# Attention with landmarks and a SiLU layer on one core: first loads reordered, two turns moved, a cast split, a new plan

## The chip, the core and the metric

The kernel runs on one core of a Trainium2 chip. Time is device time in microseconds (us) of one launch on that core, input and output in the chip's memory. The core has five engines that work in parallel, each strictly through its own list of instructions: TensorE (PE, matrix products, with a separate track PEld for weight loads), VectorE (DVE), ScalarE (ACT), GpSimd (POOL) and SyncE (SP, here only transfers). Where an engine's next instruction waits on a semaphore, everything behind it on that engine waits too.

## The reference

```python
batch, n_heads, seq, head_dim = (8, 8, 576, 64)      # q, k, v
n_tokens, d_model, d_ff = (4608, 512, 2048)          # w_in, w_out
q_lm = q.reshape(B, H, m, S // m, D).mean(axis=3)    # m = 32 landmarks, S // m = 18
k_lm = k.reshape(B, H, m, S // m, D).mean(axis=3)
A  = sm(q, k_lm)          # softmax over scale * a @ b^T
Bm = sm(q_lm, k_lm)
C  = sm(q_lm, k)
Z  = Bm^T / (norm1(Bm) * norminf(Bm) + 1e-06)
for _ in range(6):
    Z = 2 * Z - Z @ Bm @ Z
x = A @ Z @ C @ v         # per head; heads side by side: 512 columns
h = x @ w_in
out = (h * sigmoid(h)) @ w_out
```

All of it in float32; the kernel works in bfloat16 with float32 sums.

## The kernel before, in words

The eight batches run one after the other, overlapped. For each batch the kernel loads q, k and v (casting to bf16 on the way), sums 18 rows into each landmark (`landmarks`), turns q and k so that the head dimension lies on partitions (`turn`), and makes the three score matrices (`scores_b`, `scores_c`, `scores_a`). exp(C) (`pc`) is transposed to `pt` and multiplied by v (`values`); six Newton steps (`steps`, `steps_x`) with that product give z (`z_of`, tile `zt`). `mix` multiplies z by w_in into M (tile `m`), which is cast from PSUM; so the wide product x @ w_in is A^T times M (`layer1`, PSUM tiles h0 and h1, SiLU by ACT). `layer2` multiplies by w_out in tiles of 128 rows, 16 products each, into o0 and o1; ACT copies each to `ost` and SP stores it.

No list of instructions is written by hand. Every step is a node of a plan (class `_Plan`, L37) with an engine, a cost, a priority and the nodes it depends on; the planner goes through time and gives each engine, of the nodes it holds to be ready, the one with the lowest priority number. `SHIFT` (L21) adds to priorities by name and batch. `FLAGS` (L26) says which engine takes a step: letters D, A, P stand for DVE, ACT, POOL, E for TensorE, S for ACT in two halves. The lists so made are fixed in the program; on the chip the real times count, not the planner's.

What the change touches:

- Loads. All go through POOL (`load_w_in` L359, `load_w_out` L370, `load` L378). The first ones follow the list `FIRST` (L30, walked at L1124): k, q, v of batch 0, quarter 0 of w_in (w01), k and q of batch 1, the rest of w_in (w12, w24), the four slabs of w_out (o0 to o3), v of batch 1. An issue waits until the load eight places earlier has landed, and POOL waits with it. In the program that was built, batch 1's q stands before its k, and the slabs of w_out come right after w24.
- A's softmax in `top_a` (L652), `exps_a` (L695) and `weights_a` (L987): each of two halves (512 and 640 columns) gets a maximum on DVE, a subtraction on DVE or POOL (L663), exp on ACT (L706), a sum and reciprocal on DVE, a product on POOL or DVE (L1004, the norm) and a transpose on DVE into `at` (L1008). For batch 0 the 640 subtraction and both norms are POOL's.
- `turn` (L477): for batches 0 to 3 four DVE transposes (L488, L495); for batches 4 to 7 two transfers on SP's queue (L481), first q then k. From batch 4 on exp(C) is also turned by SP (L792).
- `mix` (L942): for batch 0 chunk 0 goes through h0, chunks 1 to 3 through o0 and o1, and each chunk is cast by two DVE instructions (L975).
- `landmarks` (L404): 'E' sums by 18 products with the identity on PE and one cast; else POOL adds a tree of five (L442). From batch `ts` = 4 on the tree waits for the subtractions of the batch before.
- PE's lists are filled with `layer2` products wherever the planner sees room.

Of the kernel before, what the change touches and what calls it, by code (L numbers as in the profile page):

```python
# [19 lines left out]

SHIFT = {'DVE gx t 3': 2.5, 'DVE qT qn 3': -0.5, 'DVE lmT lm 3': 3.5, 'PE t gx 3': 3, 'DVE crec csum 3': -0.25, 'DVE asum ea 0': -0.5, 'POOL kn 1': -0.5, 'DVE at ea 3': 2, 'DVE asum ea 2': 2.5, 'ACT ea s 3': 1.0, 'PE t qn 0': -1, 'DVE bs t 3': -2.5, 'POOL qn 3': -1, 'DVE m h 0': -1.75, 'POOL kn 3': -1.0, 'POOL bmd bm 0': -0.25, 'POOL kn 2': -3.0, 'DVE pt h 1': 2, 'PE t gx 2': -1, 'PE t xp 0': -0.25, 'PE t lmT 1': 0, 'ACT ea s 1': 1, 'ACT xp h 0': -2, 'PE t bt 1': 2, 'ACT lm h 2': 0.5, 'DVE bm t 3': 0.25, 'DVE m h 1': 1, 'PE t gc1g 0': 0.5, 'DVE cmax h 2': 0.25, 'PE h m 0': -2, 'DVE bsum t 1': -0.25, 'PE o g 0': 0.5, 'DVE at ea 2': 0.5, 'PE o g 2': 2, 'DVE kT kn 0': -1, 'POOL bmd bm 2': 1, 'PE t lmT 2': 0.5, 'DVE n t 1': -2, 'PE t kn 0': 1, 'DVE at ea 0': 3, 'POOL vn 1': 2, 'PE h m 2': -0.25, 'PE o lmT 0': 1, 'PE h pt 1': -0.5, 'DVE rn n 2': 2, 'PE o g 1': 2, 'DVE gc0t t 1': 0.5, 'PE t lmT 3': -0.5, 'PE t bt 0': 0.25, 'ACT ost3b o 3': 0.25, 'PE h zt 0': 1, 'DVE lmT lm 2': -2, 'DVE n t 2': 1, 'POOL qn 1': -0.5, 'DVE bt gc0t 1': 2, 'DVE brec bsum 1': -0.25, 'DVE cneg cmax 3': -1, 'ACT t bs 2': -1, 'DVE bmax t 2': -1.25, 'POOL bmd bm 3': -0.25, 'DVE gc0g t 1': 0.25, 'POOL ea arec 2': 2, 'POOL tree kn 3': 2, 'DVE lmT lm 1': -2.5, 'POOL qn 0': -0.25, 'DVE gc1g t 1': 0.25, 'DVE bs t 2': 1.0, 'DVE bsum t 3': 0.5, 'DVE n t 5': -0.25, 'PE t qn 1': 0.5, 'DVE bm t 7': -1, 'PE h pc 0': -0.25, 'PE t kn 1': -0.5, 'DVE s h 6': -2, 'DVE bmax t 7': -0.5, 'ACT pc h 6': 0.5, 'PE h lmT 3': -1, 'PE t bm 3': 0.75, 'DVE rn n 1': 0.0, 'DVE bt bm 2': 0.25, 'DVE amax s 7': -0.5, 'ACT pc h 1': -0.5, 'POOL qn 4': -0.5, 'DVE pt h 2': -1.75, 'DVE kT kn 2': -0.5, 'DVE pt h 4': 0.25, 'DVE n t 3': 1, 'DVE bmd t 0': -2, 'DVE bs t 1': 1, 'ACT m h 5': 1, 'DVE bmax t 1': -2, 'ACT ost o 7': 1, 'DVE crn crec 0': -0.5, 'PE t gc0t 1': 1.0, 'PE t xp 2': -1.5, 'PE t gx 5': 2, 'DVE gx t 2': 1, 'PE o g 3': 2, 'DVE pt h 7': -1, 'DVE crec csum 7': -1, 'PE h zt 3': -1, 'DVE rn n 3': 1, 'PE t gx 6': 1, 'ACT t bs 5': -1, 'POOL kn 4': 0.25, 'DVE at ea 1': 1, 'DVE bt bm 3': 2, 'ACT g h 1': 0.5, 'ACT ost o 0': 0.5, 'ACT ost3b 7': -2, 'DVE qT qn 2': -2, 'ACT m h 4': -0.5, 'DVE at ea 4': -2, 'PE h m 3': -1, 'DVE arec asum 2': -1, 'DVE ident s 0': 1, 'DVE xp gx 2': 1, 'PE t gc1g 1': -2, 'POOL tree qn 6': 1, 'DVE asum ea 6': 0.5, 'DVE gd gx 5': 2, 'DVE kT kn 3': 0.25, 'DVE crn crec 1': 0.25, 'PE h zt 2': 0.5, 'PE t gx 7': -2, 'PE t gc0t 0': 2, 'ACT t bs 3': -0.25, 'ACT g h 2': 2, 'DVE btd bt 4': 2, 'POOL lm tree 3': 0.5, 'DVE gc0g t 0': 1, 'POOL tree 3': -2, 'PE o g 5': 1, 'ACT t bs 1': 0.25, 'ACT ost o 2': 0.5, 'DVE qT qn 0': 1, 'DVE s o 1': -2, 'POOL tree qn 5': 2, 'DVE arec asum 3': 2, 'DVE cneg cmax 6': 2, 'DVE brec bsum 0': -0.25, 'ACT lm t 0': -2, 'ACT ea s 2': 2, 'ACT ea s 5': -2, 'DVE gd gx 2': -0.5, 'DVE asum ea 5': 2, 'POOL ea arec 1': 2}  # L21

FLAGS = {'st0': 'DDDAAA', 'st1': 'DAAADD', 'pt0': 'SS', 'pt1': 'AA', 'sub0': 'DP', 'sub1': 'DP', 'mul0': 'PP', 'mul1': 'PD', 'lm1': 'EE', 'lm2': 'EE', 'lz': 1, 'tb': 4, 'ts': 4, 'gb': 2, 'pb': 4}  # L26
TB, PB, GB = FLAGS['tb'], FLAGS['pb'], FLAGS['gb']


FIRST = ['k0', 'q0', 'v0', 'w01', 'k1', 'q1', 'w12', 'w24', 'o0', 'o1', 'o3', 'o2', 'v1']  # L30

XM = 0.21

# [180 lines left out]
def kernel(  # L214
# [143 lines left out]

    def load_w_in(lo, hi):  # L359
        def f():  # L360
            for qd in range(2):
                G.dma_start(
                    out=w_in_sb[64 * qd:64 * qd + 64, :, 512 * lo:512 * hi],
                    in_=moe_w_in[256 * qd:256 * qd + 256,
                                 512 * lo:512 * hi].rearrange(
                        "(h d) f -> d h f", d=D))
        return P.add("POOL", 1.4, f, w=[f"w_in{c}" for c in range(lo, hi)],
                     dma=[1.3 * (hi - lo)] * 2, prio=-5)

    def load_w_out(ci):  # L370
        def f():
            G.dma_start(
                out=w_out_sb[:, 4 * ci:4 * ci + 4, :],
                in_=moe_w_out[512 * ci:512 * ci + 512, :].rearrange(
                    "(c p) f -> p c f", p=128))
        P.add("POOL", 0.7, f, w=[f"w_out{ci}"], dma=[2.6], prio=-0.5)

    def load(t, src, b):  # L378
        if t == "v":
            def f():  # L380
                for t3 in range(3):
                    G.dma_start(  # L382
                        out=nat[t][b % 2][32 * t3:32 * t3 + 32].rearrange(
                            "p h j d -> p h (j d)"),
                        in_=src[b].rearrange("h (l t j) d -> t l h (j d)",
                                             t=3, j=6)[t3])
            P.add("POOL", 2.0, f, w=[f"{t}n{b % 2}"], dma=[0.95] * 3,
                  prio=-5 if b == 0 else -0.5)
            return
# [4 lines left out]
        def f():  # L394
            G.dma_start(out=dst, in_=rows.rearrange("(c p) n -> p c n", p=128))  # L395
        P.add("POOL", 0.75, f, w=[f"{t}n{b % 2}"],
              dma=[2.8], after=gate, prio=-5 if b == 0 else -0.5)


    HALF = ((0, 8), (8, SEG))  # L400
    TS = FLAGS["ts"]
    subs = {}

# [73 lines left out]
    def turn(b):  # L477
        p2 = b % 2
        if b >= TB:
            for t, dst in (("k", kTd), ("q", qTd)):  # L480
                P.add("SP", 2.3, lambda t=t, dst=dst: nc.sync.dma_start_transpose(  # L481
                    out=dst.rearrange("p a i n -> p (a i) n"),
                    in_=nat[t][p2].rearrange("p a i d -> p (a i d)")),
                    r=[f"{t}n{p2}"], w=[f"{t}T.0", f"{t}T.1"], prio=-1, lat=4.7)
            return
        for qd in range(2):
            def f(qd=qd):
# [3 lines left out]
                        "p (t c) w -> p t c w", c=6))  # L491
            dve(576, f, r=[f"kn{p2}"], w=[f"kT.{qd}"], prio=3 if b else 0.2)
        for qd in range(2):
            def f(qd=qd):
# [3 lines left out]
                        "p i w -> p (i w)"))  # L498
            dve(576, f, r=[f"qn{p2}"], w=[f"qT.{qd}"], prio=3 if b else 0.9)

# [431 lines left out]

    def copy_m(b, ci):
        dst = m_sb[b % 2][:, :, 512 * ci:512 * ci + 512]
        if ci % 2:
            dve(1024, lambda: V.tensor_copy(out=dst, in_=h_ps[1]), r=["h1"],  # L936
                w=[f"m{b % 2}.{ci}"], prio=0.1)
        else:
            act(1024, lambda: A.copy(out=dst, in_=h_ps[0]), r=["h0"],  # L939
                w=[f"m{b % 2}.{ci}"], prio=-1)  # L940

    def mix(b):  # L942

        p2 = b % 2
        for ci in range(4):
# [27 lines left out]
            if b == 0 and ci:  # L973
                for qd in range(2):
                    dve(512, lambda qd=qd, dst=dst, tgt=tgt: V.tensor_copy(  # L975
                        out=dst[:, qd], in_=tgt[qd]), r=[ks[qd]],
                        w=[f"m{p2}.{ci}"], prio=1)
            else:
# [8 lines left out]
    def weights_a(b):  # L987

        a3 = b % 3
        for hf, (i0, i1) in enumerate(HALF):  # L990
# [15 lines left out]
                    2).to_broadcast((128, 2 * (p1 - p0), LM, 2)), op=OP.mult),  # L1006
                r=[f"arec{hf}"], w=[f"ea{hf}"], prio=0.92 if on_dve else -1)
            dve(n // 2, lambda ev=ev, p0=p0, p1=p1: V.transpose(  # L1008
                out=at_sb[a3][:, :, p0:p1].bitcast(FP).rearrange(
# [5 lines left out]
    def layer1(b, part=range(NDC)):  # L1015
# [5 lines left out]
        if b == 0:  # L1021
            for hf, (i0, i1) in enumerate(HALF):
                t0, t1 = 32 * i0, 32 * i1
                n = t1 - t0
                for d2 in range(NDC // 2):
                    hp = h_ps[d2 % 2]

                    def f(d2=d2, hp=hp, t0=t0, t1=t1, n=n):
                        for j in range(2):
                            dc = 2 * d2 + j  # L1030
                            for qd in range(2):
# [3 lines left out]
                    pe(4 * _mm_cost(n), f, r=([f"m0.0{d2}d", f"m0.0{d2}a"] if d2 < 2 else  # L1035
                                               [f"m0.{d2 // 2}"]) + [f"at{a3}.{hf}"],
                       w=[f"h{d2 % 2}"], mode="full", prio=1, ni=8, hold=1)
# [84 lines left out]
    for b in range(B):  # L1122
        loads += [("k", k, b), ("q", q, b), ("v", v, b)]
    for n, x in enumerate(FIRST):  # L1124
        if n == 2:
            constants()
        if x[0] == "w":
            load_w_in(int(x[1]), int(x[2]))
        elif x[0] == "o":
            load_w_out(int(x[1]))  # L1130
        else:
            load(*loads[3 * int(x[1]) + "kqv".index(x[0])])
    for step in SEQ:
# [5 lines left out]
        if step[0] in "ES":  # L1139
# [6 lines left out]
            else:  # L1146
# [12 lines left out]
                weights_a(b)  # L1159
                z_of(b)  # L1160
        if step[0] in "EX":
            if b:
# [56 lines left out]
```

## Time and profile before

| | |
|---|---|
| three runs | 264.89, 265.57, 266.40 us, median 265.57 |
| profiled execution | 266.55 us |
| its span, first to last instruction | 264.8 us |
| mean granted TensorE clock | 0.971 |
| PE busy | 243.5 us (92%) |
| ACT, DVE, POOL busy | 161.6, 149.9, 124.1 us |
| written by DMA | 35.03 MB, mean 132 GB/s |
| `layer2` products, 555 recorded | 133.7 us |
| `layer1` products of 288, 512 recorded (with two other shapes) | 76.5 us |

The three runs lie within 0.6% of each other. The profiled execution is 0.98 us above the median. PE is the engine that is nearly always busy; from 235.5 us to the end it does nothing but `layer2`. In the lines below, a row of the timeline has the start in us, the duration, engine, line, operation, tiles, shape and count, and in brackets how long the engine stood idle before and what ended that.

### The profile page before, as it was taken

How to read it: one execution, taken by the hardware profiler on the slowest of the kernel's cores; microseconds unless marked ns; L12 is line 12 of the kernel's file. 1: busy time of each engine (PE TensorE's matmuls, PEld its weight loads, DVE VectorE, ACT ScalarE, POOL GpSimd, SP SyncE). 2: the span in 40 equal slices, each digit the busy share in tenths (PEclk: the TensorE clock that was granted, in tenths of full speed). 3: DMA queues.
4: the chain of work that ended last, by engine and by line, in shares of the span. 5: the costliest groups of instructions: out<-in, count | busy, mean ns of one | idle time of the engine just before them, and what ended most of it. 6: DMA issues, size and time to landing. Idle time of an engine off the chain costs nothing.

```text
span 264.8 us, 6634 instructions
## 1 busy us (share of the span) xinstructions
PE 243.5 (92%) x2702; PEld 138.4 (52%) x2739; DVE 149.9 (57%) x394; ACT 161.6 (61%) x275; POOL 124.1 (47%) x141
## 2 busy tenths in 40 slices
PE   5868799999799999999999989998999999999993
PEld 3733455644564466445744556435743664654452
DVE  4696853888994995486548644596369723000000
ACT  2173379843986588658865966386769786861111
POOL 8525617949431599259943995189422300000000
PEclk9985799999999999999999999999999999999998
DMA  6999999999596867188995999894215111013334
GB/s 95 198 202 211 206 209 207 207 223 222 97 174 120 136 126 129 40 167 181 165 198 108 179 169 214 144 180 98 59 40 102 42 41 42 0 40 78 72 69 102
DMA packets 47838, 35.03 MB, mean 132 GB/s; under 512 B 29248, under 2 KB 38720, under 8 KB 47808
## 3 DMA queue, kind: packets, MB, share of 16 engines
q0 software_dynamic: 14624, 18.35, 41.4%
q1 hardware_dynamic: 33104, 16.19, 30.8%
q8 instruction: 21, 0.34, 0.5%
q10 hardware_dynamic: 80, 0.07, 0.1%
q14 instruction: 9, 0.07, 0.1%
HBM read 36.70 MB, written 9.44 MB: 174 GB/s over the span
## 4 chain that ended last, share of the span: by engine, by line
PE 68%; DMA 12%; POOL 6%; DVE 5%; issue 4%; ACT 3%; ACTq 0%; POOLq 0%; DVEq 0%
PE o L244 39%; PE h L244 27%; DMA w_in_sb<-in_moe_w_in_dram 7%; DMA vn<-in_v_dram 3%; PE t L244 3%; POOL tree L442 3%; DMA lmdT<-lmd 2%; DMA pt<-pc 1%; POOL vn L382 1%; DVE cmax L587 1%; DVE pt L809 1%; ACT ost L1086 1%; ACT g L1055 1%; DVE s_sb L640 1%; POOL qn L395 1%
## 5 line engine op out<-in xcount | busy, mean ns | idle before, releaser
L244 PE MATMUL o<-w_out_sb,g 128*128 128x512 bf16 (+1 forms) x555 | 133.7, 373 | 3.3 <-issue 2.1
L244 PEld LDWEIGHTS <-g 128*128 128x128 bf16 x592 | 52.7, 98 | 52.5 <-issue 7.9
L1055 ACT ACTIVATE g<-h 128x576 bf16<-128x576 f32 x112 | 67.6, 651 | 17.4 <-PE h L244 17.2
L244 PE MATMUL h<-at,m 128*128 128x288 bf16 (+2 forms) x512 | 76.5, 290 | 1.5 <-DVE pt L809 0.8
L244 PEld LDWEIGHTS <-m 128*128 128x128 bf16 x512 | 49.4, 99 | 26.4 <-issue 2.9
L1086 ACT COPY ost<-o 128x512 f32<-128x512 f32 (+1 forms) x37 | 21.2, 573 | 45.1 <-PE o L244 44.6
L663 POOL TENSOR_TENSOR s_sb<-s_sb,amax 128x640 f32<-128x640 f32 (+1 forms) x14 | 16.2, 1170 | 47.7 <-DVE amax L657 46.7
L442 POOL TENSOR_TENSOR tree<-tree 128x512 f32<-128x512 f32 (+2 forms) x30 | 24.5, 816 | 2.0
L936 DVE CAST m<-h 128x1024 bf16<-128x1024 f32 x14 | 17.1, 1218 | 13.5 <-PE h L244 8.9
L1004 POOL TENSOR_TENSOR ea<-ea,arec 128x512 bf16<-128x512 bf16 (+1 forms) x15 | 17.0, 1147 | 9.3 <-DVE arec L999 9.3
L939 ACT CAST m<-h 128x1024 bf16<-128x1024 f32 x14 | 14.2, 1012 | 7.5 <-PE h L244 7.3
L906 DVE SCALAR_TENSOR_TENSOR gx<-gx,t 128x192 bf16<-128x192 bf16 x30 | 10.5, 352 | 13.2 <-PE t L244 13.0
L706 ACT ACTIVATE ea<-s_sb 128x512 bf16<-128x512 f32 (+1 forms) x16 | 13.0, 845 | 4.7 <-POOL s_sb L663 4.1
L712 DVE TENSOR_TENSOR gd<-gx,t 128x256 bf16<-128x256 bf16 x36 | 15.1, 419 | 1.2
L382 POOL DMA_DIRECT2D vn<-in_v_dram x24 | 14.1, 593 | 1.3 <-PE t L244 1.0
L587 DVE TENSOR_REDUCE cmax<-h 128x1 f32<-128x576 f32 x16 | 11.8, 749 | 4.1 <-PE h L244 4.0
L1038 ACT ACTIVATE g<-h 128x512 bf16<-128x512 f32 (+1 forms) x16 | 9.8, 648 | 6.9 <-PE h L244 6.9
L688 ACT ACTIVATE pc<-h,cneg 128x576 bf16<-128x576 f32 x16 | 11.7, 733 | 3.6 <-DVE cneg L590 3.5
L995 DVE TENSOR_REDUCE asum<-ea 128x16 f32<-128x512 bf16 (+1 forms) x16 | 11.8, 742 | 1.5 <-ACT ea L706 1.4
L442 POOL TENSOR_TENSOR tree<-qn 128x1152 f32<-128x1152 bf16 x5 | 11.9, 2375 | 0.9 <-DMA qn<-in_q_dram 0.7
L442 POOL TENSOR_TENSOR tree<-kn 128x1152 f32<-128x1152 bf16 x5 | 11.9, 2372 | 0.0
L657 DVE TENSOR_REDUCE amax<-s_sb 128x16 f32<-128x512 f32 (+1 forms) x16 | 11.3, 733 | 0.0
(124 smaller groups left out, 258.1 us busy)
## 6 DMA issues: line engine op xcount, KB each, us to landing
out_dram<-ost SPq DMA_DIRECT2D x70, 128.0 KB, 2.4
kn<-in_k_dram POOLq DMA_DIRECT2D x8, 576.0 KB, 10.6
qn<-in_q_dram POOLq DMA_DIRECT2D x8, 576.0 KB, 9.1
vn<-in_v_dram POOLq DMA_DIRECT2D x24, 192.0 KB, 7.8
w_out_sb<-in_moe_w_out_dram POOLq DMA_DIRECT2D x4, 512.0 KB, 17.7
w_in_sb<-in_moe_w_in_dram POOLq DMA_DIRECT2D x4, 256.0 KB, 11.6
w_in_sb<-in_moe_w_in_dram POOLq DMA_DIRECT2D x2, 512.0 KB, 16.4
out_dram<-ost SPq DMA_DIRECT2D x3, 64.0 KB, 2.0
```

What stands on the lines that cost most here:

```text
L244: nc.tensor.matmul(out=out_ap, lhsT=lhsT, rhs=rhs, start=start, stop=stop, tile_position=tp, skip_group_check=True)
L382: G.dma_start(out=nat[t][b % 2][32 * t3:32 * t3 + 32].rearrange("p h j d -> p h (j d)"), in_=src[b].rearrange("h (l t j) d -> t l h (j d)" ...
L442: lambda: G.tensor_tensor(out=o, in0=a, in1=c, op=OP.add),
L587: dve(576, lambda qd=qd: V.tensor_reduce(out=cmax[:, qd:qd + 1], in_=h_ps[qd][:, :, 0:SH], axis=AX.XY, op=OP.max), r=[f"h{qd}"], w=[f"cmax ...
L663: E.tensor_tensor(out=sv, in0=sv, in1=mv.unsqueeze(2).to_broadcast((128, 2 * (i1 - i0), LM)), op=OP.subtract),
L706: act(1.3 * n, lambda eo=eo, ei=ei: A.activation(out=eo, in_=ei, func=AF.Exp, scale=sc / SEG), r=[f"s{hf}"] + gate, w=[f"ea{hf}"], tab="ex ...
L712: P.add("DVE", _dve(256), lambda: V.tensor_tensor(out=gd, in0=src[:, :, 0:LM].unsqueeze(2).to_broadcast((128, 2, 4, LM)), in1=heads_ps.uns ...
L936: dve(1024, lambda: V.tensor_copy(out=dst, in_=h_ps[1]), r=["h1"], w=[f"m{b % 2}.{ci}"], prio=0.1)
L939: act(1024, lambda: A.copy(out=dst, in_=h_ps[0]), r=["h0"], w=[f"m{b % 2}.{ci}"], prio=-1)
L1004: lambda ev=ev, p0=p0, p1=p1, E=V if on_dve else G: E.tensor_tensor(out=ev, in0=ev, in1=arec[:, p0:p1].rearrange("p i a j -> p (i a) j").u ...
L1055: act(576, lambda dc=dc, hp=hp: A.activation(out=g[:, dc, c0:c0 + S].rearrange("p (a n) -> p a n", a=2), in_=hp[:, :, 0:SH], func=AF.Silu) ...
L1086: act(n, lambda ob=ob, c0=c0: A.copy(out=os_[:, c0:c0 + n], in_=ob[:, 0:n]), r=[ok], w=[sk] if c0 == 0 else [sk + "b"], prio=0.5)
```

## The change

Six things are changed, in one edit:

1. `FIRST` is cut in two by '|'. The part behind it (w_out and v of batch 1) is added later, with a dependency on batch 0's first norm of A (`norm0[0]`), and its slabs are numbered in order.
2. Batch 1's four DVE transposes depend on batch 0's z (`late`).
3. For batches 4 to 7, k's transfer in `turn` depends on the last written `pt` of both halves, that is, of the batch before.
4. M of batch 0: chunks 2 and 3 are cast by ACT for o0 and by DVE for o1 (`m0`: 'DDADAD'; chunk 1 stays DVE). The tile's name is split so that each half can be waited for.
5. Flags: `pt0` 'AS', `pt1` 'DA' (batch 1's first half of pt is DVE's, was ACT's), `lm2` 'PE' (batch 2's k landmarks by POOL's tree, q's stay on PE), `ts` 3 (batch 3's tree waits for batch 2's subtractions as well).
6. The plan: 4 entries of SHIFT are gone, 18 are new and 6 have other values; the planner's margin XM ahead of a `layer1` product goes from 0.21 to 0.06, its cost of a q or k load from 2.8 to 2.9.

```diff
-FLAGS = {'st0': 'DDDAAA', 'st1': 'DAAADD', 'pt0': 'SS', 'pt1': 'AA', 'sub0': 'DP', 'sub1': 'DP', 'mul0': 'PP', 'mul1': 'PD', 'lm1': 'EE', 'lm2': 'EE', 'lz': 1, 'tb': 4, 'ts': 4, 'gb': 2, 'pb': 4}
+FLAGS = {'st0': 'DDDAAA', 'st1': 'DAAADD', 'pt0': 'AS', 'pt1': 'DA', 'sub0': 'DP', 'sub1': 'DP', 'mul0': 'PP', 'mul1': 'PD', 'lm1': 'EE', 'lm2': 'PE', 'lz': 1, 'm0': 'DDADAD', 'tb': 4, 'ts': 3, 'gb': 2, 'pb': 4}
...
-FIRST = ['k0', 'q0', 'v0', 'w01', 'k1', 'q1', 'w12', 'w24', 'o0', 'o1', 'o3', 'o2', 'v1']
-
-XM = 0.21
+FIRST = ['k0', 'q0', 'v0', 'w01', 'k1', 'q1', 'w12', 'w24', '|', 'o0', 'o1', 'o2', 'o3', 'v1']
+
+XM = 0.06
...
         P.add("POOL", 0.75, f, w=[f"{t}n{b % 2}"],
-              dma=[2.8], after=gate, prio=-5 if b == 0 else -0.5)
+              dma=[2.9], after=gate + list(after), prio=-5 if b == 0 else -0.5)
...
-                    r=[f"{t}n{p2}"], w=[f"{t}T.0", f"{t}T.1"], prio=-1, lat=4.7)
+                    r=[f"{t}n{p2}"], w=[f"{t}T.0", f"{t}T.1"], prio=-1, lat=4.7,
+                    after=[P.last_w[f"pt{x}.0"] for x in range(2)] if t == "k" else [])
             return
+        late = [P.last_w["zt0"]] if b == 1 else []
...
-            dve(576, f, r=[f"kn{p2}"], w=[f"kT.{qd}"], prio=3 if b else 0.2)
+            dve(576, f, r=[f"kn{p2}"], w=[f"kT.{qd}"], after=late, prio=3 if b else 0.2)
...
                 for qd in range(2):
-                    dve(512, lambda qd=qd, dst=dst, tgt=tgt: V.tensor_copy(
-                        out=dst[:, qd], in_=tgt[qd]), r=[ks[qd]],
-                        w=[f"m{p2}.{ci}"], prio=1)
+                    if FLAGS["m0"][2 * ci - 2 + qd] == "D":
+                        dve(512, lambda qd=qd, dst=dst, tgt=tgt: V.tensor_copy(
+                            out=dst[:, qd], in_=tgt[qd]), r=[ks[qd]],
+                            w=[f"m{p2}.{ci}{qd}"], prio=1)
+                    else:
+                        act(512, lambda qd=qd, dst=dst, tgt=tgt: A.copy(
+                            out=dst[:, qd], in_=tgt[qd]), r=[ks[qd]],
+                            w=[f"m{p2}.{ci}{qd}"], prio=0.5)
...
+            norm0.append(P.last_w[f"ea{hf}"])
...
                 z_of(b)
+                for x in FIRST[FIRST.index("|") + 1:]:
+                    first_load(x, [norm0[0]])
```

What the plan makes of it, read from the two built programs: POOL's loads are now k0, q0, v0, w01, k1, q1, w12, w24, then k and q of batch 2, then the norm of A's first half and the 640 subtraction, then the four slabs of w_out, the second norm, v of batch 1. On PE, four of batch 0's sixteen `layer1` steps (a step is four products) stand before the product with w24, where before none did; 8 w_out products instead of 10 come before batch 1's C scores, 34 instead of 32 before batch 1's first mix, 228 instead of 232 before batch 5's scores, and the same 304 before batch 6's. On SP, exp(C)'s two transfers of batches 4 to 6 now come before the next batch's k transfer, not behind it.

## The prediction

> **What bounds the kernel now.** I read the page's slices first, then sums by stretch, then the timeline where PE stands or runs slowly, then the chain of waits. The slices:
>
> ```profile
> PE   5868799999799999999999989998999999999993
> PEclk9985799999999999999999999999999999999998
> ```
>
> After the fifth slice (33 us) PE is at 9 nearly everywhere, so the end is the sum of PE's work plus its idle time, and a change counts where it removes PE work, removes PE idle time, or brings useful PE work forward into the slow front. By stretch (PE busy first, granted clock and DMA last):
>
> ```profile
> 20.00:30.00 10.00, 7.48 (x73) 3.54 (x61) 7.76 (x18) 3.15 (x6) 6.26 (x8) 0.62 1.17 208
> 30.00:40.00 10.00, 9.31 (x110) 5.43 (x111) 6.22 (x16) 6.02 (x11) 2.40 (x4) 0.83 1.23 207
> 60.00:70.00 10.00, 8.66 (x171) 4.53 (x170) 9.02 (x24) 5.78 (x11) 6.58 (x8) 1.00 0.87 187
> 150.00:160.00 10.00, 8.70 (x109) 5.95 (x109) 4.42 (x12) 7.27 (x14) 9.76 (x12) 1.00 0.96 184
> 170.00:180.00 10.00, 9.05 (x108) 3.62 (x108) 9.15 (x23) 8.51 (x14) 8.01 (x7) 1.00 1.07 181
> ```
>
> The front has idle PE, a clock of 0.62 and 0.83, and loads that run at 207 GB/s without pause. Later three stretches lose 1.34, 1.30 and 0.95 us. Why the front is slow, from the timeline:
>
> ```profile
> 14.71 0.76 POOL L372 DMA_DIRECT2D w_out_sb<-in_moe_w_out_dram  x1 [1.10 <-DMA w_in_sb<-in_moe_w_in_dram]
> 19.78 0.74 POOL L372 DMA_DIRECT2D w_out_sb<-in_moe_w_out_dram  x1 [3.04 <-DMA qn<-in_q_dram]
> 22.52 0.74 POOL L372 DMA_DIRECT2D w_out_sb<-in_moe_w_out_dram  x1 [2.00 <-DMA kn<-in_k_dram]
> 23.28 1.27 POOL L663 TENSOR_TENSOR s_sb<-s_sb,amax 128x640 f32<-128x640 f32 x1
> 24.51 1.05 POOL L1004 TENSOR_TENSOR ea<-ea,arec 128x512 bf16<-128x512 bf16 x1
> 24.58 0.92 ACT L706 ACTIVATE ea<-s_sb 128x640 bf16<-128x640 f32 x1 [4.07 <-POOL s_sb L663]
> 30.45 0.41 PE L244 MATMUL o<-w_in_sb,zt 64*32 64x512 bf16 x7 [1.75 <-DMA w_in_sb<-in_moe_w_in_dram]
> 30.79 1.73 PE L244 MATMUL h<-at,m 128*128 128x256 bf16 x8
> ```
>
> The subtraction's maximum was ready at 20.36 (DVE L657, 19.55 plus 0.81) and the norm's reciprocal at 20.51, but POOL stood in w_out's issues until 23.26. So `layer1` begins only at 30.79, behind w24, and its first eight products take 1.73 us where eight at full clock take 1.05 (34.78). The late stretches:
>
> ```profile
> 144.36 3.60 SPq L481 DMA_TRANSPOSE kT<-kn  x1
> 149.97 2.66 SPq L792 DMA_TRANSPOSE pt<-pc  x2
> 153.25 0.36 PE L244 MATMUL t<-vn,pt 96*32 96x64 bf16 x24 [0.62 <-DVE at L1008]
> 154.24 0.36 PE L244 MATMUL t<-vn,pt 96*32 96x64 bf16 x24 [0.63 <-DMA pt<-pc]
> 162.99 4.66 DMA lmdT<-lmd
> 180.03 0.36 PE L244 MATMUL t<-vn,pt 96*32 96x64 bf16 x24 [0.47 <-DMA pt<-pc]
> ```
>
> exp(C) of batch 5 is done at 147.46 and 148.19 (ACT), but its turn starts at 149.97 behind k's turn. The fifth row is from the chain of waits: batch 6's landmarks reach PE at 167.65, after POOL has worked almost without gap since 143.21.
>
> **Part 1, the front (changes 1, 2, 4, lm2).** k and q of batch 2 take the two issue slots at 14.71 and 16.00. POOL is then free at 16.7 and takes the norm at about 20.3 (1.05), the subtraction until 22.65, then w_out's four issues until some 25.9, each waiting for a load that has landed by then. DVE's first `at` transpose moves from 29.93 to 21.5; zt, held at 22.96 behind a k transpose that waited for its load, comes at 22.0, the mix at 22.5. ACT's exp ends at 24.6, the table load (1.28) at 25.9. So PE can do four `layer1` steps between 25.4 and 30.4, where it now did identity products and stood 1.75. w24 lands at 30.4 as before: the same bytes precede it. After it twelve steps are left instead of sixteen. ACT now sets the pace: its last SiLU ends at 44.2 today; with two 0.55 us casts put between the SiLUs and eight of 0.65 for the second half I get 41.9.
>
> Then w_out decides. Loads drain in order: the issues at 32.70 and 35.24 were released by slabs 1 and 2, so 2.54 us per 512 KB, and slab 4 lands at 35.24 + 2 x 2.54 = 40.3. Ahead of it now stand two 576 KB loads, 2.86 each: 46.0. PE wants the fourth slab at 45.6 in the new order (it got there at 46.9 before) and stands 0.5 us. The Trainium skill, "DMA: Bandwidth & Descriptors", section "Anatomy of one DMA", gives about 2.0 us plus bytes/436 GB/s for one such transfer; by it alone the slab would be there before 30 and the sum 0.5 us better. The trace says 17.5 to 19.0 us from issue to landing, because the queue is full, and I go by that.
>
> Batch 1's chain from there: second exp(C) 46.0 instead of 48.1, ACT and DVE share its pt (0.75 and 0.93 side by side, where ACT took 1.52), six steps at the present spacing, v of batch 1 landing at 46.0 + 2.86 = 48.9 just before `values` at 49.6, mix at 54.25 instead of 56.04. That is 1.8 us, and inside it are the 18 k products that leave PE (three rows of six, 0.49 to 0.51: 1.5 us; POOL's tree, 5.4 us, fits between 33.9 and 39.4, where POOL now idles). Two more w_out products are done by then, 2 x 0.22 = 0.44. Ends for this part: no gain if the fourth slab lands 2.2 us later than I have it; 3.0 if PE stays at clock 1.0 and the slab does not bind.
>
> The clock: it fell to 0.50 for 31 to 34 after a PE that was busy 1.25 of 3 us (28 to 31). With PE busy from 24.5 to 30 I take 1.0 from 28 on. The Trainium skill, "TensorE: Matmul & The Clock Gate", section "What's actually happening", has the clock fall only after a whole idle window of about 3.4 us; here it fell with 1.75 us of idle, so the row is the harsher guide. If it falls anyway, about 3 us at half clock cost 1.5, of which w_out's wait hides 0.5.
>
> **Part 2, batches 2 and 3.** `ts` 3 takes the tree (5 us) out of the way of batch 2's subtractions (63.96, ready at 63.05). But ACT's order puts A's exp before exp(C): pt0 0.2 and pt1 0.4 later, of which I count 0.3 on PE. Batch 3's landmarks then end on POOL near 80.5, and lmT at 82 for scores at about 84: nothing, covered by 2 us; without the cover each us late is one on PE.
>
> **Part 3, SP (change 3).** Batch 5: exp(C)'s turn starts at 147.5 and lands by 151.7, before PE needs it, so the 0.62 + 0.63 go. But PE then meets lmdT, POOL's chain, which begins with batch 5's scores (140.30) and ends 27.4 us later whatever PE does. The new order brings those scores four w_out products forward (228 against 232) and does them behind: 4 x 0.22 = 0.88, allowed because the landmarks for 140.30 were there 1.5 us early (135.55 plus 3.3). So 0.88 of 1.25 is kept. Batch 6: turn at 173.9 instead of 175.11, 0.35 + 0.47 of waiting gone and some 0.03 behind it, 0.85; batch 7's landmarks land at about 192 for use at 194.9, so nothing takes it back. k's turn, now later, lands near 157 for use at 170; POOL's next k load into that buffer waits for the turn of a batch earlier. Ends: 0 and 2.1.
>
> **Sum.** -1.8 - 0.44 + 0.3 - 0.88 - 0.85 = -3.7 on the profiled 266.55 (span 264.8 and 1.75 around it): 262.9. The median shown is 0.98 lower than that execution, so 265.57 - 3.7 = 261.9.
>
> **Rivals.** (B) The chains in the front keep the old time: v of batch 1, which lands 2.9 us later than before (46.0), or the late clock, holds batch 1's mix near 55.5. Front -1.0, the rest as above: 265.57 - 1.0 + 0.3 - 1.7 = 263.2, or 264 if part 3 also gives half. For it: DMA is saturated until 66; against it: 0.7 us of slack at v. (C) The lead is given back at landmark points, as it is at batch 6: POOL's 20 to 27 us chains are as long as PE's stages. If batches 3 to 7 are set by them, only the 1.7 of part 3 could vary and the time is about 265. Against: slack of 1.5 to 2 us at batches 4, 5 and 7. (D) Slower: w_out in PE's list. From 39 to 47 PE's list holds w_out products in between, so a late slab stops everything behind it, scores and steps of batch 1 too. Each us past 46.0 is one us of time; from 3.7 us late (49.7) the kernel loses, and at 51.5 it is 265.57 + 1.8 = 267.4. For it: the slabs are issued 8 us later behind POOL work, and six more loads follow them closely; against: 2.7 MB are still queued when they are issued, so the rate should hold. (E) All of the front's 3.0 and part 3's 2.1: 265.57 - 4.8 = 260.8.
>
> **Numbers.** Forecast 0.50 (its own range 260.9 to 263.4), B 0.17, C 0.12, D 0.16, E 0.05. A difference of under 0.5% (1.33 us) can't be told from none here. Faster: A, E and most of B, 0.68; the same: C and a little of B, 0.15; slower: D and 0.01 of C, 0.17. The range 260.2 to 266.8 leaves out about 0.17, nearly all of it D.
>
> **What would show it.** Right: POOL's first norm at about 20.3 and w_out's issues behind 22.6; eight to sixteen `layer1` products before 30.4; clock 1.0 in 31 to 35; ACT's last batch 0 SiLU near 42; batch 1's mix near 54.3; no PE wait for pt at batches 5 and 6; batch 6's scores near 164.5. Wrong: a PE wait for w_out over 1 us, or w24 landing past 31; a mix of batch 1 at 56 or later; PE idle before lmdT products at batch 3, 5 or 7.

## The result, and the profile after

The changed kernel takes 275.07 us (median of four runs, 273.69 to 276.62) where the kernel before, measured beside it, takes 265.99 (264.89 to 266.79). The ratio is 1.0346, with a 95% interval of 1.0277 to 1.0415. The forecast was 261.9, with a range up to 266.8: wrong in sign and in size. The profiled execution (273.69 us, the fastest of the four) has a span of 272.0 us. The medians lie 9.08 us apart, the two profiled executions that are compared below 7.20 us in span: before's lies above its median, and the changed kernel's is the fastest of its four.

PE and its granted clock in 40 slices of 6.8 us, changed kernel:

```profile
PE   5678899898999999999979994399999999999994
...
PEclk9965899999999999999999999579999999999999
```

Two slices, from 163 to 177 us, have a PE at 4 and 3 and then a clock at 5. Nothing like it stood in the profile before, and PE's whole busy time is the same 243.5 us. The same place by stretch (busy time of PE first, granted clock, DMA share and GB/s last):

```profile
160.00:170.00 10.00, 6.48 (x37) 3.08 (x35) 1.36 (x4) 2.13 (x4) 1.86 (x3) 0.98 1.38 139
170.00:180.00 10.00, 5.85 (x67) 2.13 (x69) 4.03 (x10) 2.49 (x4) 1.05 (x1) 0.51 0.85 151
```

From 166 to 174 us PE, DVE, ACT and POOL all but stand, while the DMA engines are busy, until 172 at least. The timeline tells what was issued, and what PE stood for:

```profile
152.79 6.42 SPq L482 DMA_TRANSPOSE kT<-kn  x1
...
152.96 0.76 POOL L396 DMA_DIRECT2D kn<-in_k_dram  x1
153.70 0.71 POOL L396 DMA_DIRECT2D qn<-in_q_dram  x1
154.40 1.74 POOL L383 DMA_DIRECT2D vn<-in_v_dram  x3
...
162.05 3.77 SPq L459 DMA_TRANSPOSE lmdT<-lmd  x1
...
173.81 0.23 PE L244 MATMUL t<-lmdT 64*32 64x32 bf16 x8 [7.28 <-DMA lmdT<-lmd]
```

And the DMA issues of 150 to 165 us, each with its time from issue to landing at the end of the line:

```profile
kn<-in_k_dram POOLq DMA_DIRECT2D x1, 576.0 KB, 11.8
qn<-in_q_dram POOLq DMA_DIRECT2D x1, 576.0 KB, 14.3
vn<-in_v_dram POOLq DMA_DIRECT2D x3, 192.0 KB, 16.3
...
kT<-kn SPq DMA_TRANSPOSE x1, 20.2
lmdT<-lmd SPq DMA_TRANSPOSE x1, 11.7
```

k's turn of batch 6, which part 3 put behind exp(C)'s turns, is issued at 152.79, at the same moment as the load of k, q and v of batch 7 (1.77 MB). It lands at 173.0, 20.2 us after its issue; the same transfer took 5.5 us before. lmdT of batch 6 is behind it on SP's queue and lands at 173.8. PE stands 7.28 us for it, and its clock is 0.50 from 170 to 179, so for some 5 us after PE works again.

Cut at points that PE passes in every kernel (its first mix product of batch 1, then the first product with each batch's landmarks), the spans can be compared stage by stage:

| stage on PE, us | before | after | difference | forecast |
|---|---|---|---|---|
| start to mix of batch 1 | 56.04 | 54.95 | -1.09 | -1.8 |
| to batch 3's scores | 29.77 | 29.31 | -0.46 | -0.44 + 0.3 |
| to batch 4's scores | 26.97 | 26.97 | 0 | 0 |
| to batch 5's scores | 27.52 | 28.01 | +0.49 | -0.88 |
| to batch 6's scores | 27.39 | 34.57 | +7.18 | 0 |
| to batch 7's scores | 26.59 | 28.29 | +1.70 | -0.85 |
| to the end | 70.52 | 69.90 | -0.62 | 0 |
| sum | 264.80 | 272.00 | +7.20 | -3.7 |

The forecast's 0.88 stands at batch 5: four w_out products fewer were to bring these scores forward (the profiles have 66 in that stage, 70 before), and POOL's chain was to keep the stage behind it at 27.4.

### The profile page after: what moved, and what is told of

Same layout as the page of the kernel before. It is cut to its first block, busy times and chain, and to the rows that moved or that the text cites. A ratio compares the mean times of both kernels' runs of the same rounds, so it can differ in the third digit from the quotient of the medians.

```text
span 272.0 us, 6604 instructions
## 1 busy us (share of the span) xinstructions
PE 243.5 (90%) x2686; PEld 136.6 (50%) x2721; DVE 149.6 (55%) x393; ACT 161.7 (59%) x274; POOL 129.7 (48%) x146
## 4 chain that ended last, share of the span: by engine, by line
PE 62%; DMA 14%; POOL 9%; DVE 8%; issue 4%; ACT 1%; POOLq 0%; ACTq 0%; DVEq 0%
PE o L244 36%; PE h L244 23%; DMA lmdT<-lmd 6%; DMA w_in_sb<-in_moe_w_in_dram 5%; POOL tree L443 5%; PE t L244 3%; DMA vn<-in_v_dram 3%; DVE asum L1007 1%; DVE pt L812 1%; POOL vn L383 1%; DVE cmax L590 1%; POOL lmd L443 1%; POOL qn L396 1%; POOL kn L396 1%; DVE s_sb L643 1%
## 5 line engine op out<-in xcount | busy, mean ns | idle before, releaser
L244 PE MATMUL o<-w_out_sb,g 128*128 128x512 bf16 (+1 forms) x557 | 135.8, 378 | 3.4 <-issue 2.4
L244 PEld LDWEIGHTS <-g 128*128 128x128 bf16 x592 | 53.2, 98 | 54.9 <-issue 10.9
L1068 ACT ACTIVATE g<-h 128x576 bf16<-128x576 f32 x112 | 67.4, 652 | 14.6 <-PE h L244 14.5
L443 POOL TENSOR_TENSOR tree<-tree 128x512 f32<-128x512 f32 (+2 forms) x33 | 27.0, 818 | 2.0
L909 DVE SCALAR_TENSOR_TENSOR gx<-gx,t 128x192 bf16<-128x192 bf16 x30 | 10.5, 349 | 12.8 <-PE t L244 12.7
L443 POOL TENSOR_TENSOR tree<-kn 128x1152 f32<-128x1152 bf16 x6 | 14.2, 2367 | 0.0
L638 DVE STREAM_TRANSPOSE s_sb<-h 128x512 f32<-128x512 f32 (+1 forms) x8 | 5.8, 758 | 11.4 <-PE h L244 11.4
## 6 DMA issues: line engine op xcount, KB each, us to landing
qn<-in_q_dram POOLq DMA_DIRECT2D x8, 576.0 KB, 10.8
```

The source lines that it names most:

```text
L244: nc.tensor.matmul(out=out_ap, lhsT=lhsT, rhs=rhs, start=start, stop=stop, tile_position=tp, skip_group_check=True)
L443: lambda: G.tensor_tensor(out=o, in0=a, in1=c, op=OP.add),
L1068: act(576, lambda dc=dc, hp=hp: A.activation(out=g[:, dc, c0:c0 + S].rearrange("p (a n) -> p a n", a=2), in_=hp[:, :, 0:SH], func=AF.Silu) ...
```

## The experiments

Most of them leave the plan as it is and move one named step in the finished lists, so that every other list keeps its order. This was added for it:

```diff
+    def put(order, names, after):    # names: the steps to move, behind the last of `after`
+        at = {n.name: n for n in order if n.name}
...
     with tc.manual_schedule():
-        for n in P.schedule():
+        order = P.schedule()
+        put(order, ['kT6'], ['pt51'])          # one such line for each move
+        for n in order:
```

kT6 is k's turn of batch 6, pt51 the second turn of exp(C) of batch 5, lmdT6 the landmark transfer of batch 6, kn7, qn7 and vn7 the loads of batch 7.

**1. Is it this transfer, and the load that it meets?** Four kernels: the changed one with kT6 back where it was, with POOL's loads of batch 7 behind batch 6's landmark sums, with kT6 one place earlier (ahead of the two stores), and the kernel *before* with only kT6 moved back.

```diff
+        put(order, ['kT6'], [])                          # e1, behind scores C of batch 5
+        put(order, ['kn7', 'qn7', 'vn7'], ['lmdq6'])     # e2
+        put(order, ['kT6'], ['pt51'])                    # e3
+        put(order, ['kT6'], ['vn7'])                     # e4, in the kernel before
```

> The changed kernel with one transfer moved: k's turn of batch 6 goes back to right behind q's turn, ahead of exp(C)'s turns, as before the change; no other list is touched. Theory 1 (k's turn at 152.8 shares the DMA engines with the 1.73 MB load of batch 7 that POOL issues from 153.0, and the landmark transfer lmdT waits behind it on SP's queue): k's turn lands in 5 to 6 us from about 144, lmdT in 4 to 5 us, batch 6's scores at 166 to 168 instead of 173.8, the 1.25 us wait for pt of batch 5 is back, and the time is 264 to 267. Rival A (lmdT itself is starved by that load, whoever is ahead of it): lmdT still takes 10 to 12 us, scores at 173 or later, 272 or more.

> The changed kernel with POOL's issues of k, q and v of batch 7 moved behind batch 6's landmark sums; k's turn stays where the change put it. Theory 1: nothing shares the engines with k's turn, it lands in 5 to 6.5 us (by 159), POOL's sums end 3.2 us earlier (158), lmdT lands by 163.5 and PE meets it without a wait or with one under 0.5 us; scores of batch 6 at 164 to 165, time 261.5 to 264. Rival B (k's turn is slow behind exp(C)'s turn for a reason of its own): it takes 15 us or more again, 270 or more.

> The changed kernel with k's turn of batch 6 right behind exp(C)'s turns, ahead of the two stores: it is issued at about 150.0 instead of 152.8, 3 us ahead of batch 7's loads. Theory 1: the part that is through before 153 is fast, the rest is starved; it lands between 155 and 168, and batch 6's scores come between 167 and 172, time 265 to 271. Rival B: the same 20 us, scores near 171 to 174, 272 or more.

> The kernel before with one transfer moved: k's turn of batch 6 goes behind exp(C)'s turns and the four stores, so it is issued at about 155, when batch 7's loads (issued from 153.85) are running. Theory 1: it takes 10 us or more and lands at 165 to 172, lmdT (issued at 163) lands at 168 to 173 instead of 167.7, and the time is 267 to 272 though the waits for pt of batch 5 are gone. Rival C (the loss needs another part of the change): k's turn lands in 6 us, scores at 166.5 to 167.7 and the time is 264 to 266.

| | time, us | ratio to before | kT6 issued | loads from | kT6 lands after | lmdT6 |
|---|---|---|---|---|---|---|
| e1 | 265.78 | 0.9987 (0.9952 to 1.0023) | 145.27 | 155.73 | 4.5 | 5.0 |
| e2 | 267.79 | 1.0073 (1.0036 to 1.0110) | 153.15 | 159.17 | 4.7 | 10.8 |
| e3 | 266.01 | 0.9996 (0.9973 to 1.0019) | 150.62 | 153.57 | 5.4 | 6.1 |
| e4 | 275.38 | 1.0327 (1.0279 to 1.0375) | 152.71 | 152.86 | 20.4 | 11.7 |

The last four columns come from the profiled execution; e1's is its longest (268.12 us).

e4 decides. One transfer moved in the old kernel, nothing else, and all of the loss is there, more than the 267 to 272 us that I expected. Its timeline, DMA issues and waits of PE (100 to 200 us):

```profile
152.71 2.37 SPq L481 DMA_TRANSPOSE kT<-kn  x1
...
152.86 0.76 POOL L395 DMA_DIRECT2D kn<-in_k_dram  x1
```

```profile
kT<-kn SPq DMA_TRANSPOSE x1, 20.4
lmdT<-lmd SPq DMA_TRANSPOSE x1, 11.7
```

```profile
PE t L244 <- DMA lmdT<-lmd: 8.6, 1, 8.6
```

e1 and e3 take the loss away, so it needs nothing else of the change. e3 came at the good end of a wide expectation: a start 2.95 us ahead of the loads is not half a cure but nearly a whole one (5.4 us). e2 was a miss in time (261.5 to 264 expected): kT6 is quick, as expected, but lmdT6, issued at 159.26 together with the moved loads (159.17), is now the one that waits, 10.8 us, and lands at 170.1 instead of by 163.5. So the collision isn't special to k's turn. Rivals A, B and C of these four runs are out.

**2. Loads held back until lmdT has landed.** The three loads of batches 6 and 7 go behind the landmark sums, and a tiny POOL sum that reads lmdT holds them there (it writes two columns of the tree's scratch, which the next tree overwrites).

```diff
+        hold(order, 5); put(order, ['kn6', 'qn6', 'vn6'], ['hold5'])
+        hold(order, 6); put(order, ['kn7', 'qn7', 'vn7'], ['hold6'])
```

> The changed kernel with POOL's loads of batches 6 and 7 moved behind the landmark sums of batches 5 and 6, and held there by a tiny POOL sum that reads lmdT, so that no load runs while lmdT of these batches or k's turn of batch 6 does. Theory 1 (the loss is made by transfers that turn data while a load runs): lmdT of batches 5 and 6 lands in about 2.5 us, k's turn of batch 6 in 4.6 to 5.5 us, PE waits for neither (1.2 us and 7.3 us in the changed kernel); batch 6's scores near 164.5; time 261.5 to 264. Rival D (the waits only move: q of batch 6 lands late, its turn blocks SP's queue, or POOL stands too long): 265 to 269 with a new PE wait of 2 us or more.

> The kernel before with the same two holds. k's turn of batch 6 still goes ahead of exp(C)'s, so the wait for pt of batch 5 (1.25 us) stays, and PE met lmdT there with 0.2 us of waiting at most. Theory 1: little to gain, 264.5 to 266. If it comes to 263 or less, the gain of the run beside it isn't the change's.

Both were misses: 273.07 us, ratio 1.0286 (1.0243 to 1.0328), and 272.12, ratio 1.0249 (1.0207 to 1.0291). lmdT is quick now (2.4 to 2.5 us, once 4.3), but rival D of e5 came: there q of batch 6 lands late, so q's turn is issued at 147.36 instead of 139.86, exp(C)'s turns stand behind it on SP's queue until 153.91, and PE stands for them:

```profile
156.74 0.51 PE L244 MATMUL t<-vn,pt 96*32 96x64 bf16 x24 [5.19 <-DMA pt<-pc]
```

e6 has the same, with a wait of 5.51 us.

**3. Is the profile before typical, and what do the other parts give?**

> The kernel before, profiled once more, for the front. If the profile that the prediction was made from is typical, the granted clock is 0.5 again in 31 to 35 us and batch 1's mix comes at 56.0 (within 0.2). If the half clock falls elsewhere in each execution, as in the run with k's turn of batch 6 late (same lists up to 145 us, mix at 54.84), it comes anywhere from 54.8 to 56, and the front's gain of 1.1 us that the changed kernel's profile shows is within that.

> The changed kernel without the dependency of k's turn on pt, planned anew: parts 1, 2, 4, 5, 6 alone. Theory 1: no loss is left; with the front's and batch 6's gains given back at lmdT of batch 5 and at pt of batch 5, the time is 264.5 to 266.5. The prediction's own sum for these parts was -1.8 - 0.44 + 0.3 = -1.9, which would be 263.5 to 264.2.

e8 drops `after=[...pt...] if t == "k"` from `turn` and plans anew. e7 came at 55.98, so the profile is typical. But with the later runs the old front was seen seven times: five times the mix came at 55.94 to 56.05, with a granted clock of 0.59 to 0.74 in 30 to 34 us, and twice (e4, e6) at 54.84 and 55.07, with a clock of 1.00 and 0.99 there. The changed front, seen 13 times, always has 0.88 or more there and comes at 54.95 to 55.58. One line of the sums by stretch for each, before and e4, the same lists:

```profile
30.00:34.00 4.00, 3.55 (x38) 2.22 (x39) 2.65 (x9) 1.50 (x3) 1.69 (x3) 0.62 1.24 206
```

```profile
30.00:34.00 4.00, 3.81 (x55) 2.41 (x49) 3.10 (x10) 2.35 (x5) 1.54 (x3) 1.00 1.24 205
```

On the means (55.71 and 55.16) the front gains 0.55 us, and what it gains is one half-clock stretch that the old order doesn't always have. e8 takes 266.87 us, 1.0044 (1.0013 to 1.0074): without part 3 the loss is gone, but the -1.9 us that I gave to the rest isn't there.

**4. When does k's turn pass?** The same transfer, still later.

```diff
+        put(order, ['kT6'], ['lmdT6'])     # e9; e10 in the kernel before; e12 in e8's plan
+        put(order, ['kT6'], ['lmdq6'])     # e11, ahead of lmdT6
```

> The changed kernel with k's turn of batch 6 one step further back than the change put it: behind lmdT, issued at about 163, ten us after batch 7's loads began. Theory 1 (a turning transfer that enters the queue together with a load is served only with the load's end; once the load is nearly through it passes): lmdT lands at 166 to 168, k's turn at 168 to 170, batch 6's scores at 166.5 to 168, no wait for pt of batch 5, time 264 to 265.8. Rival E (k's turn may not be later than before at all): its scores C wait 2 us or more for it, or lmdT still takes 10 us, 268 or more.

> The kernel before with that same single move. Theory 1: the wait for pt of batch 5 (1.25 us) goes and lmdT is the bound instead; scores of batch 6 at 166.5 to 167.5, time 264.3 to 265.8, against 275.4 where the same transfer stood at 152.7. Rival E: 268 or more.

> The changed kernel with k's turn of batch 6 behind the store that follows it but ahead of lmdT, issued at 158 to 159, five us after batch 7's loads began and while they run. Theory 1 in its strong form (starved until the load is through, wherever it enters): it lands with or behind the loads, 165 to 169, lmdT behind it at 168 to 172, scores of batch 6 at 169 to 172, time 267 to 271. In its weak form (only a transfer that enters with the load's first packets is starved): it lands in 5 to 7 us, lmdT at 167 to 168, time 264.5 to 266.

> The plan without part 3 (266.87 us), with k's turn of batch 6 behind lmdT. There pt of batch 5 made PE wait 1.04 us and lmdT of batch 5 none. Theory 1: that wait goes, scores of batch 6 at 166 to 167.5, time 264.5 to 266, and the best of the versions if the front holds. Rival F (the lead is given back at lmdT of batch 6, whose landmarks POOL finishes at 161.5 whatever PE does): scores at 167.3 or later and no gain against the run without this move, 266 to 267.

e9: 266.60 us, 1.0006 (0.9965 to 1.0046). e10: 269.15, 1.0102 (1.0070 to 1.0133). e11: 271.9, 1.0205 (1.0145 to 1.0265, two executions). e12: 268.12, 1.0067 (1.0023 to 1.0111). kT6 took 5.6 us in e9, issued 10.5 us after the first load; 5.2 in e10; 10.9 in e11, issued 5.2 us after it. That is the strong form of theory 1: a turn that meets the load is slow until the load is through. e9's time is above the 264 to 265.8 that I expected. e10 and e12 were misses as times. In e10 scores of batch 6 came where I expected (167.2); in e12 they came at 167.7, where rival F had them: PE stands 0.63 us for lmdT, so the lead is given back there. In both q's and k's turns of batch 7 were late in SP's list ahead of pt of batch 6, for which PE stood 1.69 + 0.52 and 1.73 + 0.48 us. The changed order, which has k's turn behind pt there too, paid 0.28 us there in e9: part 3's order serves at batch 6, and at batch 5 it puts the turn beside the load.

**5. Out of the load's way, and the length of the wait.** Only v's three issues of batches 6 and 7 are held behind lmdT; k's and q's loads stay. e13 has kT6 as in e3, e15 where the change put it.

```diff
+        put(order, ['kT6'], ['pt51'])                     # e13, e18
+        hold(order, 5); put(order, ['vn6'], ['hold5'])    # e13 to e18
+        hold(order, 6); put(order, ['vn7'], ['hold6'])
+        put(order, ['kT6'], ['pt51']); put(order, ['kT7'], ['pt61'])    # e17, in the kernel before
```

> The changed kernel with k's turn of batch 6 right behind exp(C)'s turns (as in the run where that was the only edit) and, new, v's three issues of batches 6 and 7 moved on POOL behind the landmark sums and held until lmdT has landed, by a tiny POOL sum that reads it; k's and q's loads stay. Theory G (the lead is given back at lmdT, because v's issues cost POOL 1.74 us in that chain and v's bytes share the engines with lmdT): no wait at batch 5 (stage from batch 4's scores to batch 5's 27.0 instead of 28.0), lmdT of batch 6 lands by 165.5, stage to batch 6's scores 26.2 to 27.5 instead of 28.9, time 262 to 264. Rival H (the other parts bring nothing): the stages stay at 28 and 28.9 or a wait for something else comes, 265.5 to 267.

> The kernel before with v of batches 6 and 7 held in the same way. Theory G: lmdT wasn't waited for here by more than 0.2 us, pt of batch 5 is still waited for (1.25 us), so the stage from batch 5's scores to batch 6's goes from 27.4 to 26.5 to 27.4 at best: 264.5 to 266. If it gains as much as the changed kernel with this edit, the change has no part in it.

> The changed kernel with v held as above and k's turn of batch 6 where the change put it, so that it enters with 1.15 MB of load (k and q of batch 7) instead of 1.73. If the starvation lasts as long as the load: k's turn lands 12 to 15 us after its issue instead of 20.2, lmdT behind it at 165.5 to 168, time 263 to 267. If its length has nothing to do with the bytes: 18 us or more again, lmdT at 171 or later, 270 or more.

> The plan without part 3 (266.87 us) with v held as above; k's turn of batch 6 goes ahead of exp(C)'s. Theory G: stage from batch 5's scores to batch 6's 26.8 to 27.6 instead of 28.4 (the wait for pt of batch 5, 1.04 us, stays), time 264 to 265.8. Rival H: 266 or more.

> The kernel before with the two moves of the best version: k's turns of batches 6 and 7 right behind exp(C)'s turns of the batch before, v of batches 6 and 7 held until lmdT has landed. Theory I (the rest of the change has a share: 0.46 us in the stage from batch 1's mix to batch 3's scores, 0.6 us after batch 7's scores, 0 to 1 us in the front): stages 29.8, 27.0, 27.5, 27.5 to 28.2, 26.2 and 70.2 to 70.6, time 265 to 266.2. Theory J (it has none): 263.8 to 264.8, the same as the run beside it.

> The best version once more, beside the run before: 263.8 to 264.8, with stages 55.0, 29.3, 27.0, 26.7 to 27.0, 28.1, 26.2 and 69.9.

| | time, us | ratio to before |
|---|---|---|
| e13, changed | 264.32 | 0.9948 (0.9918 to 0.9978) |
| e18, the same again | 263.29 | 0.9896 (0.9858 to 0.9933) |
| e17, before, k's turns and v moved | 264.30 | 0.9955 (0.9927 to 0.9983) |
| e14, before, v moved alone | 269.09 | 1.0104 (1.0047 to 1.0161) |
| e16, changed without part 3, v moved | 268.91 | 1.0079 (1.0040 to 1.0118) |
| e15, changed, v moved, kT6 at its place | 267.35 | 1.0039 (1.0007 to 1.0071) |

e13, e18 and e17 are faster than both kernels, by 0.5 to 1.0% against the one before. SP's and POOL's lists in e13, and what PE still waits for between 100 and 200 us:

```profile
146.24 2.61 SPq L795 DMA_TRANSPOSE pt<-pc  x2
148.95 3.42 SPq L482 DMA_TRANSPOSE kT<-kn  x1
...
151.71 0.76 POOL L396 DMA_DIRECT2D kn<-in_k_dram  x1
...
159.09 1.22 SPq L459 DMA_TRANSPOSE lmdT<-lmd  x1
```

```profile
PE t L244 <- DMA pt<-pc: 1.2, 2, 0.7
```

kT6 is 2.76 us ahead of the load and lands in 6.5 us, lmdT6 is issued 3 us earlier than in the changed kernel, and PE waits for no lmdT. e14 and e16 fell short of what I gave them for the reason of e10: qT and kT of batch 7 stand ahead of pt of batch 6, now beside v's load (qT 8.8 us in e14), and PE stands 2.23 + 1.00 us. In e15 the load that kT6 meets has a third fewer bytes, and kT6 lands after 14.6 us instead of 20.2.

e16's time is what rival H gave it (266 or more), and e17's, the old lists with the two moves, is what theory J gave it (263.8 to 264.8); both say that the rest of the change has no share. Against them stands e18, 1.0 us below e17.

Spans by stage of the runs that are compared by them (from the mix of batch 1 to the scores of batches 3 to 7, then to the end):

| | mix b1 | b3 | b4 | b5 | b6 | b7 | end |
|---|---|---|---|---|---|---|---|
| before | 56.04 | 29.77 | 26.97 | 27.52 | 27.39 | 26.59 | 70.52 |
| e4 | 54.84 | 29.77 | 26.97 | 27.73 | 34.44 | 27.94 | 70.61 |
| e10 | 56.03 | 29.77 | 26.97 | 27.52 | 26.91 | 29.59 | 70.61 |
| e14 | 56.05 | 29.76 | 26.97 | 27.52 | 27.74 | 29.00 | 70.16 |
| e17 | 55.94 | 29.77 | 26.97 | 27.51 | 25.77 | 27.01 | 70.13 |
| after | 54.95 | 29.31 | 26.97 | 28.01 | 34.57 | 28.29 | 69.90 |
| e2 | 55.04 | 29.31 | 26.97 | 28.21 | 30.54 | 26.78 | 69.85 |
| e3 | 55.58 | 29.31 | 26.97 | 28.00 | 28.94 | 25.56 | 69.84 |
| e8 | 55.58 | 29.31 | 26.97 | 27.30 | 28.42 | 26.69 | 69.93 |
| e9 | 55.08 | 29.32 | 26.97 | 28.83 | 27.99 | 25.97 | 69.94 |
| e13 | 54.96 | 29.32 | 26.97 | 26.74 | 28.11 | 26.15 | 69.95 |
| e18 | 55.16 | 29.31 | 26.97 | 26.96 | 28.03 | 26.96 | 69.91 |

## Why the prediction was wrong

**The step that failed** is in part 3: "k's turn, now later, lands near 157 for use at 170". The 5 us from issue to landing came from rows in which the transfer had the DMA engines nearly to itself. I looked at who needs k's turn, and at the buffer that it frees, but not at what else enters the DMA engines at its new time. The trace before had the answer: POOL's loads of batch 7 start at 153.85 and take some 11 us, and lmdT at 162.99, at their end, had already taken 4.66 us. The two stages that were to gain 0.88 together measured +0.49 and +7.18, and the slow clock behind the stall turned the next one from -0.85 into +1.70 (without the stall, e3 has 25.56 there, the kernel before 26.59 and 26.13 in e7: -0.6 to -1.0, so that term itself was about right). What was right in part 3 is that the waits for pt of batches 5 and 6 go: the changed kernel has neither.

**The front** (-1.8) measured -1.09 against the one profile, and 0.55 on the means. What was right: POOL's first norm at 19.86 (said: 20.3), w_out's issues from 22.07 (22.6), 16 `layer1` products before w24's part, clock 1.0 in 31 to 35, the last SiLU of batch 0 at 42.50 (42), w_out's fourth slab landing at 45.65 (46.0). Three steps were off:

```profile
25.46 1.89 PE L244 MATMUL h<-at,m 128*128 128x256 bf16 x8
...
29.06 1.35 PE L244 MATMUL h<-at,m 128*128 128x256 bf16 x8
...
48.92 0.49 PE L244 MATMUL h<-qn,ident 128*128 128x128 bf16 x6 [0.89 <-DVE pt L812]
```

The clock was 0.50 until 29, not 1.0 "from 28 on": eight products take 1.89 us instead of 1.05. The four steps (16 products) still fit ahead of w24's part at 30.67, and w24 had landed at 30.27, so this cost 0.4 us at most. The wait for w_out's fourth slab (0.5 us at 46) did not come, though the slab landed where it was forecast, so the loads' queue was not the bound that I and the prediction's rival D made it. And pt of batch 1 was late: ACT does A's exp first (46.51, 0.91 us) and DVE starts its half at 47.93, so PE stands 0.89 us, and of the 1.7 us by which the last SiLU is early, 1.1 are left at the mix.

**The two more w_out products** (-0.44) measured -0.46, in every run with the changed lists. The +0.3 for batch 2's pt did not show.

**Batch 5's scores** were to come 0.88 us earlier; the stage lost 0.49 us, and 0.5 to 1.4 in the six runs with the changed lists at that place (28.0 to 28.95). The four w_out products are gone from it, but PE stands 1.20 us for lmdT of batch 5, which takes 5.2 us there:

```profile
139.24 0.21 PE L244 MATMUL t<-lmdT 64*32 64x32 bf16 x8 [1.20 <-DMA lmdT<-lmd]
```

The prediction allowed the lead because these landmarks "were there 1.5 us early (135.55 plus 3.3)". The 3.3 is the median of the four lmdT transfers of the kernel before; the one issued at 135.55 took 4.1, so 0.65 us were free, less than the 0.88:

```profile
DMA to landing us min/median/max: 2.4/3.3/4.7
...
lmdT<-lmd SPq DMA_TRANSPOSE x1, 4.1
```

The lead is given back, as the prediction's rival C said, but at batch 5. Holding v back ends it (26.7 and 27.0 in e13 and e18, so 0.8 and 0.6 of the 0.88 are there): it is a load beside lmdT again. That the last stage, from batch 7's scores to the end, is shorter in all runs with the changed lists (69.8 to 69.95, against 70.5 to 70.6 with the old lists and 70.1 with the old lists and loads held) was not foreseen, and I did not find out why.

**The prediction's rival D**, the one on the slower side, had the right shape and the wrong place: something late in an in-order list that blocks what stands behind it. The list was SP's, the late thing k's turn, and what stood behind it was lmdT. Priced from the rows, a turn that lands with the load's end (153.85 + some 11 us of load, and its own 5 in between) would have come near 170 and lmdT behind it near 172, where PE met it at 167.7: an estimate of about 4 us slower, made afterwards from rows that I had quoted in part. Rivals B and E leave out the 0.44 that the sum counts; with it they come to 262.7 and 260.3.

**What stays open**: whether the other parts of the change bring anything. Measured side by side, the best version has 0.9896 (0.9858 to 0.9933) and the old lists with the same two moves 0.9955 (0.9927 to 0.9983); the intervals touch, and e13's 0.9948 lies beside the second.

## What to carry to other kernels

Before a transfer is moved, list what every queue feeds to the DMA engines around its new time, not only who waits for it. A turning transfer that meets a large load is about as late as the load, and so is all that stands behind it on its queue; issued 3 us ahead of the load, or 10 us after its start, it came through here in 5.2 to 6.5 us. And a stall costs more than itself where the clock falls in it: here PE worked some 5 us at half clock behind 7.28 us of standing.

## What the runs showed of the hardware

While both queues had work (156 to 169 us of the changed kernel), they moved equal numbers of packets, whatever the packets held, as if the DMA engines served one packet of each in turn. Packets, MB and busy share in single microseconds of the changed kernel (160, 161, 163 and 165 us; q0 carries POOL's loads, q1 SP's transfers):

```profile
q0 software_dynamic: 75, 0.17, 89.5%
q1 hardware_dynamic: 75, 0.02, 14.8%
...
q0 software_dynamic: 89, 0.17, 89.2%
q1 hardware_dynamic: 90, 0.02, 20.7%
...
q0 software_dynamic: 151, 0.14, 95.1%
q1 hardware_dynamic: 151, 0.04, 43.0%
...
q0 software_dynamic: 97, 0.08, 84.1%
q1 hardware_dynamic: 103, 0.03, 66.1%
```

A load's packet holds 0.8 to 2.3 KB, a turning transfer's 256 bytes (0.02 MB over 75 to 90 packets), so the turn gets a tenth to a quarter of the bytes. Alone, in e3 at 150 us, such transfers move three to seven times as many packets in a microsecond:

```profile
q1 hardware_dynamic: 520, 0.13, 63.7%
```

k's turn moves 0.59 MB (576 KB of bf16), some 2300 such packets. The load has 1360 (1.77 MB), so k's turn, one for one, is still at work when the load ends, and the wait goes with packets: 20.2 us beside the whole load, 14.6 without v, and 10.8 for lmdT of e2, which has only some 540 packets. This also fits the cure by 3 us: the load's first packets show 2 us after POOL's issue, and by then a turn issued 3 us ahead is nearly through (e3: no packet of it is left after 156). The Trainium skill, "DMA: Bandwidth & Descriptors", section "Queues, rings and completion order", states that each engine goes round its queues and takes a whole packet from one before it goes on to the next; the equal counts agree, if the profile's packets are the ones meant there.

The granted clock of the front differs between executions of the same lists: 0.59 to 0.74 in 30 to 34 us five times, 0.99 to 1.00 twice. The Trainium skill, "TensorE: Matmul & The Clock Gate", section "What's actually happening", says that the window by which the clock is judged runs freely and does not start with the kernel; the runs agree with it, and a front should be priced from several profiles, not from one.
